# Weight sums of five groups instead of three in stage one, the first gate run's operand sums on VectorE, and another order of casts and one result copy

## The chip, the cores and the metric

The kernel runs on one core of a Trainium2 chip. The metric is the device time of one execution in microseconds. A core has five engines that run their own instruction lists in order and wait for each other by semaphores: PE (TensorE, matrix multiplication), DVE (VectorE) and POOL (GpSimd) for elementwise work, ACT (ScalarE) for functions and casts, and SP (SyncE), which here only issues DMA transfers.

## The reference, cut to what matters

```
scores = cap * tanh(q @ k^T / sqrt(64) / cap)            # 8 batches, 12 heads, 448 x 448
x  = softmax(scores) @ v   -> (8, 448, 768)
xp = x shifted by one position
k  = relu((mu_k * x + (1 - mu_k) * xp) @ w_k)            # w_k 768 x 1024
v  = (k * k) @ w_v                                       # w_v 1024 x 768
r  = sigmoid((mu_r * x + (1 - mu_r) * xp) @ w_r)         # w_r 768 x 768
out = r * v                                              # (8, 448, 768)
```

The weights come as 64-bit floats and are rounded to float32 by the kernel.

## The kernel before, in words

**Stage one** goes over 48 pairs of heads, two at a time ("units", listed in `UNIT`): scores, tanh, exp, values, the mix of positions, and between them the product with w_k (L463) whose results go through a relu (L473, tile ko) into the DRAM tensor k_d. x goes to x_d. In the same units the weights w_r and w_v are rounded, block by block: the last sum of a rounding is `weight_sum` on POOL (L548), and `weight_store` writes the block to w_d in DRAM.

**Stage two** computes the gate r and v for 14 chunks of 256 positions. Each chunk has a run "r" and a run "v". A run is a fast form of a block product with seven products instead of eight (m = 0 to 6): it needs seven sums of blocks of the operand and seven of the weights. The weights make seven groups k (0 to 2 of w_r, 3 to 6 of w_v). A group has four raw blocks of 128x384 and three more that are sums, 128x2688 in all. Where the sums are made depends on NRAW: for a group k < NRAW the four raw blocks are stored in stage one, loaded (768 KB), and summed in place by four subtractions (`group_sums`) after the load; for the others `weight_sum` writes into the tile gt, `T` makes four subtractions there on POOL in stage one, and seven blocks are stored and loaded (1344 KB). NRAW is 4 before.

After the load each group is split: `group_high` casts it to the high part on ACT (L120, 128x2688), `group_low` subtracts on DVE for the low part (L607, 128x2688). The tiles are named by letters: raw groups 0 to 6 are w2A, w2C, w2E, w2I, w2K, w2H, w2M; their high parts w2B, w2D, w2F, w2J, w2L, w2K, w2O; their low parts w2G, w2A, w2C, w2E, w2I, w2N, w2H. So the high part of group 5 (w2K) takes the place of raw group 4 and can't be written before the low part of group 4 is made from it; the low part of group 6 (w2H) takes the place of raw group 5.

**The passage between the stages** is written by hand. `LAST` lists the end of stage one and `TAIL` what is done beside the last eight blocks of the w_k product (h = 0 to 7, 18 matmuls each): `l` loads a group, `p` and `d` sum it on POOL or DVE, `c` is `group_high`, `s` is `group_low`, `@n` is the work of slot n on the first operands. A slot's work: `load_x` reads mixed positions from x_d (tile xc), `mix_r` multiplies on ACT (L662) and adds on DVE (L663) into t, `square` (L668) squares the k chunk kr, `sum1`, `sum23` and `sum4` are the four operand sums of a run, `split` casts an operand on ACT (L120, tiles ro and vo) and subtracts on DVE (L699). `chain` then goes slot by slot: `product` (L711), the slot's work, and `post`, which takes a product's result out of PSUM. The first post copies the first product (m = 4, bank ps2c) to the tile cp (L722). The third product (m = 3) adds on into the same bank, so it can't start before that copy is done. cp lies where the three ko buffers were, so the copy also waits until the last stores of ko have landed. The last ko is the relu of h = 7.

Of the kernel before, what the change touches and what calls it, by code (L numbers as in the profile page):

```python
# [57 lines left out]
LAST_R = ((-6, 4), (-3, 2), (-2, 3), (0, 0), (5, 5), (8, 1), (10, 6))  # L58
LAST_V = ((-6, 4), (-4, 2), (-3, 0), (-1, 3), (0, 5), (2, 1), (4, 6))
LAST_SPLITS = ((-8, 4), (-7, 2), (-6, 0), (-4, 3), (-3, 5), (-2, 1), (0, 6))  # L60
TAIL = ("@-12 @-11 @-10 c2 s2 p3", "@-9 @-8 c3 s3 @-7", "@-6 @-5 @-4", "open c4 s4 c5", "", "", "", "")
NRAW = 4
TAIL_TAGS = ("c0", "b0", "a0", "c1", "b1", "a1")
PAD = (24, 56)
RAW_SLOTS = "ACEIKHM"
# [22 lines left out]
k_store k_store f x_high.1 x_low.1 weight_store T T T load_vl load_v.1 x_store.0 weight_load load_qk.1 x_store.1"""  # L88
LAST = """V.0 V.1 VL next gather p0 p1 c0 recip rec_store rec_load l2 s0 c1 norm.0 norm.1 K K K relu K relu k_store
mix_old.0 mix_new.0 x_high.0 x_low.0 s1 K K mix_old.1 relu k_store K mix_new.1 x_high.1 x_low.1 relu K K relu k_store  # L90
k_store x_store.0 x_store.1 d2"""


def uncut(i):
# [3 lines left out]
def f(ap):  # L98
    return ap.bitcast(F32)


class Body:
# [441 lines left out]
    def weight_sum(self, e="p"):  # L544
        for n, a, sq in self.w_sum:
            k, q = divmod(n - NWK, 4)
            out = sq if k < NRAW else self.gt[:, q]
            {"p": self.nc.gpsimd, "v": self.nc.vector}[e].tensor_add(out, f(a), sq)  # L548
# [6 lines left out]
            else:  # L555
                if k < NRAW or q != 1:
                    self.w_done.append((k, q, out))
                if k >= NRAW:
                    self.w_block += {1: [(k, 4, 4, 1, 0)], 3: [(k, 1, 7, 3, 1), (k, 5, 5, 3, 4), (k, 6, 6, 2, 5)]}.get(q, [])
# [26 lines left out]
    def group_load(self, k):  # L586
        n = 4 if k < NRAW else 7
        self.nc.sync.dma_start(self.W[k][:, 0:n], self.w_d[k][:, 0:n])
# [86 lines left out]
        k, h = {0: (0, 0), 2: (1, 0), 3: (1, 0), 1: (0, 1), 6: (1, 1)}[m]  # L675
        return t[:, k * g:k * g + g, h * P:h * P + P]

    def sum1(self, p, c):
        if p == "r":
            self.S1[p] = self.xin.tile([P, KG[p], P], F32, name="s1")  # L680
        self.nc.gpsimd.tensor_add(self.S1[p], self.block(p, c, 1), self.block(p, c, 6))  # L681

    def sum23(self, p, c):
        a11, a21 = self.block(p, c, 0), self.block(p, c, 1)
        self.sub("p", self.S1[p], self.S1[p], a11)
        self.sub("p", a21, a11, a21)

    def sum4(self, p, c):
        a12 = self.block(p, c, 2)
        self.sub("p", a12, a12, self.S1[p])  # L690

    def split(self, p, c, m):
        a = self.block(p, c, m)
# [52 lines left out]
    def runs(self):  # L746

        runs = [(p, c) for c in range(NC) for p in "rv"]
        pe, prep = {}, {}
        for n, (p, c) in enumerate(runs):  # L750
            last = p + str(c - NC + 1)
            for rel, m in dict(r0=LAST_R, v0=LAST_V).get(last, PRODUCTS):
                pe[7 * n + rel] = (n, p, c, m)
            todo = [(-23, self.load_x, (c,)), (-12, self.mix_r, (c, 0)), (-11, self.mix_r, (c, 1)), (-10, self.mix_r, (c, 2))]
            todo = todo if p == "r" else [(-23, self.load_k, (c,)), (-12, self.square, (c, 0)), (-11, self.square, (c, 1))]
            todo += [(-9, self.sum1, (p, c)), (-7, self.sum23, (p, c)), (-5, self.sum4, (p, c))]
            todo += [(rel, self.split, (p, c, m)) for rel, m in (LAST_SPLITS if last == "v0" else SPLITS)]
            for rel, fn, a in sorted(todo, key=lambda x: x[0]):
                prep.setdefault(7 * n + rel, []).append((fn, a))
        return pe, prep  # L760
# [86 lines left out]
    def run(self):  # L847
# [8 lines left out]
        with ExitStack() as outer:  # L856
            def pool(name, bufs, stack=outer, **kw):
                return stack.enter_context(tc.tile_pool(name=name, bufs=bufs, **kw))
# [57 lines left out]
            for i in range(NSTEP):  # L916
# [22 lines left out]
                if i > NPAIR + 1:  # L939
                    for h in range(2 * (i - NPAIR - 2), 2 * (i - NPAIR - 1)):  # L940
                        n = B * NF * ND * 3 - (8 - h) * 3 * ND
                        self.kpart(n, n + 3 * ND)
                        self.relu()
                        self.k_store()
                        self.tail_work(TAIL[h])
            self.k_store()
# [9 lines left out]
            self.S1["v"] = t[:, NF * CH:NF * CH + KG["v"] * P].rearrange("p (c s) -> p c s", c=KG["v"])  # L956
            self.rsp = pool("rsp", 1, reuse_waits="tile")
            self.opp["v"] = [pool("opv0", 1, reuse_waits="tile")]
            self.tail_work("s5 c6")
            self.chain(pe, -6, -1)  # L960
            self.prep[-1].reverse()
            self.preps(-1)
            self.tail_work("s6")
# [55 lines left out]
```

## Time and profile before

| | us |
|---|---|
| median of 3 runs (lowest, highest) | 922.11 (921.96, 924.5) |
| the profiled execution | 922.12 |
| its span, first to last instruction | 919.9 |
| PE busy, of the span | 889.0 (97%) |
| DVE, ACT, POOL busy | 733.8 (80%), 619.8 (67%), 435.7 (47%) |
| PE busy in 400 to 500 | 100.00 |
| PE busy in 520 to 560 | 24.10 of 40 |
| PE busy in 700 to 800 | 99.50 |

The profiled execution took as long as the median run, and 2.2 us of it lie outside its span. PE is busy almost everywhere, except at the very start and end and in one place, between 530 and 560 us, where the kernel passes from stage one to stage two.

### The profile page before, as it was taken

The page shows a single profiled execution, that of the slowest core. Times are in us where ns is not written, and L with a number is a line of the kernel's source. Part 1 is how long each engine was busy: PE and PEld are TensorE (multiplying, and loading weights), DVE is VectorE, ACT ScalarE, POOL GpSimd, SP SyncE. Part 2 cuts the span into 40 slices and gives each one's busy share as a digit, 9 for nine tenths or more (in the row PEclk, how much of TensorE's full clock was granted, in tenths as well). Part 3 has the DMA queues.
Part 4 walks back from the last instruction along what each step waited for, and adds up shares of the span by engine and source line. Part 5 has one row for each costly group of instructions (what it writes and reads, how often), then busy time and mean ns, then how long its engine had stood idle before and what let it go on. Part 6 is the DMA issues. An engine that isn't in the chain of part 4 may idle for free.

```text
span 919.9 us, 14330 instructions
## 1 busy us (share of the span) xinstructions
PE 889.0 (97%) x5046; PEld 697.8 (76%) x5046; DVE 733.8 (80%) x1102; ACT 619.8 (67%) x957; POOL 435.7 (47%) x412
## 2 busy tenths in 40 slices
PE   7999999999999999999999948999999999999997
PEld 2335557767677776667777938999999999999997
DVE  5878987878978888897955748888888888888883
ACT  7897787788797788977973455555455555645542
POOL 2443454555555565666647614434444344334440
PEclk9999999999999999999999979999999999999999
DMA  7355565566666675666757731332333223322301
GB/s 254 115 162 179 189 193 166 190 196 186 187 217 206 191 225 179 195 206 205 211 188 235 264 116 44 115 107 83 113 107 115 79 89 115 115 88 100 107 35 47
DMA packets 96698, 140.61 MB, mean 153 GB/s; under 512 B 11496, under 2 KB 86120, under 8 KB 96232
## 3 DMA queue, kind: packets, MB, share of 16 engines
q1 hardware_dynamic: 87400, 124.91, 43.6%
q10 hardware_dynamic: 9216, 14.68, 4.2%
q8 instruction: 42, 0.69, 0.3%
q14 instruction: 40, 0.33, 0.1%
HBM read 93.00 MB, written 44.15 MB: 149 GB/s over the span
## 4 chain that ended last, share of the span: by engine, by line
PE 46%; DVE 22%; ACT 13%; issue 8%; POOL 6%; DMA 3%; SPq 1%; ACTq 0%; POOLq 0%; DVEq 0%
PE kps L463 17%; PE pv L299 10%; PE s L264 10%; DVE vo L699 3%; DVE cp L742 3%; ACT vo L120 3%; DVE ro L699 3%; DVE t L663 3%; POOL t L126 3%; PE ps2a L711 2%; ACT ro L120 2%; PE pv L308 2%; ACT t L662 2%; PE s L274 2%; PE kps L320 1%
## 5 line engine op out<-in xcount | busy, mean ns | idle before, releaser
L280 ACT ACTIVATE p<-s,scl_t 128x896 f32<-128x896 f32 x144 | 139.3, 996 | 16.3 <-PE s L264 14.4
L290 ACT ACTIVATE p<-p,cap_t 128x896 f32<-128x896 f32 x144 | 145.2, 1036 | 1.9
L463 PE MATMUL kps<-xkh,wkl 128*128 128x448 f32 x384 | 143.5, 374 | 0.8 <-ACT ko L473 0.8
L345 DVE TRANSPOSE_TENSOR_REDUCE r<-p 128x28 f32<-128x896 f32 x126 | 136.0, 1093 | 6.2 <-ACT p L290 6.0
L463 PE MATMUL kps<-xkl,wkh 128*128 128x448 f32 x384 | 140.6, 366 | 0.0
L463 PE MATMUL kps<-xkh,wkh 128*128 128x448 f32 x384 | 140.3, 365 | 0.0
L299 PE MATMUL pv<-p,rv 128*64 128x448 f32 x576 | 115.1, 544 | 0.0
L463 PEld LDWEIGHTS kps<-xkh,wkl 128*128 128x128 f32 x384 | 72.0, 188 | 26.4 <-issue 13.7
L299 PEld LDWEIGHTS pv<-p,rv 128*64 128x64 f32 x576 | 38.6, 136 | 66.4 <-issue 56.6
L548 POOL TENSOR_TENSOR wsq<-wa,wsq 128x384 f32<-128x384 f32 x32 | 34.5, 1080 | 112.7 <-DVE wsq L539 112.7
L463 PEld LDWEIGHTS kps<-xkl,wkh 128*128 128x128 f32 x384 | 72.2, 188 | 8.0 <-issue 2.8
L463 PEld LDWEIGHTS kps<-xkh,wkh 128*128 128x128 f32 x384 | 72.1, 188 | 5.8
L699 DVE TENSOR_TENSOR ro<-t,ro 128x384 fp32r<-128x384 f32 x70 | 38.7, 554 | 39.9 <-ACT ro L120 38.9
L699 DVE TENSOR_TENSOR vo<-x,vo 128x512 fp32r<-128x512 f32 x63 | 57.1, 914 | 15.9 <-ACT vo L120 15.6
L126 POOL TENSOR_TENSOR qkl<-rqk,qkh 128x832 fp32r<-128x832 f32 x34 | 67.6, 1987 | 2.8
L396 DVE TENSOR_TENSOR x<-pv,r 128x448 f32<-128x448 f32 x48 | 28.2, 620 | 42.9 <-DMA r<-rec_d 42.9
L663 DVE SCALAR_TENSOR_TENSOR t<-xc,mu_r,t 128x256 f32<-128x256 f32 (+3 forms) x120 | 57.0, 527 | 0.9
L126 POOL TENSOR_TENSOR xkl<-xk,xkh 128x448 fp32r<-128x448 f32 x48 | 55.6, 1157 | 3.9
L733 ACT ACTIVATE rs<-rs 128x384 f32<-128x384 f32 x28 | 14.7, 526 | 62.7 <-DVE rs L732 62.7
L120 ACT CAST ro<-t 128x384 fp32r<-128x384 f32 x70 | 34.4, 509 | 33.4 <-POOL t L126 33.0
L681 POOL TENSOR_TENSOR s<-t 128x384 f32<-128x384 f32 x14 | 16.9, 1205 | 75.5 <-DVE t L663 75.5
L662 ACT ACTIVATE t<-xc,om_r 128x256 f32<-128x256 f32 (+3 forms) x120 | 44.6, 435 | 3.4 <-DMA xc<-x_d 3.4
(199 smaller groups left out, 2400.8 us busy)
## 6 DMA issues: line engine op xcount, KB each, us to landing
rqk<-qk SPq DMA_DIRECT2D x47, 448.0 KB
k_d<-ko ACTq DMA_DIRECT2D x64, 224.0 KB
x_d<-x SPq DMA_DIRECT2D x48, 224.5 KB
out<-cp SPq DMA_DIRECT2D x56, 192.0 KB
rv<-v SPq DMA_DIRECT2D x48, 192.0 KB
r<-rec_d SPq DMA_DIRECT2D x36, 224.0 KB
kr<-k_d SPq DMA_DIRECT2D x7, 1024.0 KB
x<-k_d SPq DMA_DIRECT2D x7, 1024.0 KB
```

Source lines behind the costliest of these rows:

```text
L120: self.nc.scalar.copy(out, x)
L126: {"p": self.nc.gpsimd, "v": self.nc.vector}[e].tensor_sub(*a)
L264: nc.tensor.matmul(s[:, h, 0:S], qk[a][p, k], qk[b][p, 0:S], start=(n == 0), stop=(n == len(terms) - 1))
L280: self.nc.scalar.activation(p32, self.S.pop((i, g))[:, :, 0:S], AF.Tanh, scale=self.scl_t)
L290: self.nc.scalar.activation(p32, p32, AF.Exp, scale=1.0 if self.maxima else self.cap_t)
L299: nc.tensor.matmul(pv[p, 0:S], v[:, g, h, :], ph[:, h, :], start=(g == 0), stop=False)
L345: self.nc.vector.tensor_reduce(out=r1[:, :, 3 if g == "L" else g], in_=self.P32[i, g].rearrange("p h (b k) -> p (h b) k", k=32), axis=mybi ...
L463: nc.tensor.matmul(self.kps[fc][:, 0:S], w, m[:, dc, :], start=first, stop=last)
L548: {"p": self.nc.gpsimd, "v": self.nc.vector}[e].tensor_add(out, f(a), sq)
L662: nc.scalar.mul(td, self.XC[:, d, j0 + o:j1 + o], self.om["r"][:, d:d + 1])
L663: nc.vector.scalar_tensor_tensor(out=td, in0=self.XC[:, d, j0 + o + 1:j1 + o + 1], scalar=self.mu["r"][:, d:d + 1], in1=td, op0=ALU.mult, ...
L699: self.nc.vector.tensor_sub(lo, a, f(hi))
```

## The change

NRAW becomes 2, so groups 2 and 3 are summed in stage one by `T` on POOL, eight subtractions of 128x384 more there. With them go 7 blocks each instead of 4 through w_d (six stores more, 192 KB each), and their loads grow from 768 to 1344 KB. The four subtractions of group 2 on DVE (`d2`) and of group 3 on POOL (`p3`) in the passage are gone. The four operand sums of the very first run (r of chunk 0) go from POOL to DVE; all other runs keep POOL. `TAIL` is written anew: the cast of group 2 (`c2`) stands at the end of `LAST`, ahead of the mixing, `c3`, `s3`, `c4`, `c5` stand in other places, and the sums of the first run are at h = 0 to 2. The cast of group 6 (`c6`) stands behind the first product and its copy instead of ahead of them.

```
-TAIL = ("@-12 @-11 @-10 c2 s2 p3", "@-9 @-8 c3 s3 @-7", "@-6 @-5 @-4", "open c4 s4 c5", "", "", "", "")
-NRAW = 4
+TAIL = ("@-12 @-11 @-10 @-9 c3 s2 @-8", "@-7 @-6", "@-5 s3 @-4", "open c4 s4", "c5", "", "", "")
+NRAW = 2
...
-k_store x_store.0 x_store.1 d2"""
+k_store x_store.0 x_store.1 c2"""
...
-    def sum1(self, p, c):
+    def sum1(self, p, c, e):
...
-        self.nc.gpsimd.tensor_add(self.S1[p], self.block(p, c, 1), self.block(p, c, 6))
+        {"p": self.nc.gpsimd, "v": self.nc.vector}[e].tensor_add(self.S1[p], self.block(p, c, 1), self.block(p, c, 6))
...
+            e = "p" if n else "v"
+            todo += [(-9, self.sum1, (p, c, e)), (-7, self.sum23, (p, c, e)), (-5, self.sum4, (p, c, e))]
...
-            self.tail_work("s5 c6")
-            self.chain(pe, -6, -1)
+            self.tail_work("s5")
+            self.chain(pe, -6, -5)
+            self.tail_work("c6")
+            self.chain(pe, -5, -1)
```

PE's list is the same in both kernels. On ACT, at the beginning of the passage (- is before, + is the change):

```order
+L120 CAST w2F<-w2E 128x2688
 L662 ACTIVATE t<-xc,om_r 128x256 x6
-L120 CAST w2F<-w2E 128x2688
-L120 CAST ro<-s_5360 128x384
 L120 CAST w2J<-w2I 128x2688
-L473 ACTIVATE ko<-kps 128x448
-L479 DMA k_d<-ko 128x448
-L120 CAST ro<-t 128x384 x2
+L120 CAST ro<-s_5345 128x384
+L120 CAST ro<-t 128x384
+L473 ACTIVATE ko<-kps 128x448
+L479 DMA k_d<-ko 128x448
```

The cast of group 2 has moved ahead of the six multiplications of the mix, and the cast of group 3 ahead of the first operand cast; the relu of h = 2 comes after two operand casts instead of one. A little further on, the relu of h = 4 and its store move ahead of the cast of group 5 (w2K).

On ACT, at the end of the passage, where flag is the load of a register and cp the first copy out of PSUM:

```order
-L473 ACTIVATE ko<-kps 128x448
-L479 DMA k_d<-ko 128x448
-L948 TENSOR_LOAD flag
+L949 TENSOR_LOAD flag
+L722 COPY cp<-ps2c 128x384
 L120 CAST w2O<-w2M 128x2688
-L722 COPY cp<-ps2c 128x384
```

The copy now stands ahead of the cast of group 6 (w2O), and one relu fewer stands between the cast of group 5 and the copy.

On DVE, at the beginning of the passage (s and t are the operand sums and the mixed operand of the first run):

```order
 L416 SCALAR_TENSOR_TENSOR xk<-x_153,mu_k,pv 128x448
-L126 TENSOR_TENSOR w2E<-w2E 128x384 x4
 L663 SCALAR_TENSOR_TENSOR t<-xc,mu_r,t 128x256 x6
+L681 TENSOR_TENSOR s_5345<-t 128x384
 L607 TENSOR_TENSOR w2C<-w2E,w2F 128x2688
-L699 TENSOR_TENSOR ro<-s_5360,ro 128x384
+L699 TENSOR_TENSOR ro<-s_5345,ro 128x384
+L126 TENSOR_TENSOR s_5345<-s_5345,t 128x384
+L126 TENSOR_TENSOR t<-t 128x3x128
+L699 TENSOR_TENSOR ro<-t,ro 128x384
+L126 TENSOR_TENSOR t<-t,s_5345 128x3x128
+L668 TENSOR_TENSOR kr<-kr 128x1024
```

The four subtractions of group 2 are gone from DVE, and the four operand sums, which POOL did before, stand between the low part of group 2 and that of group 3. Then come the low part of group 3, the third operand, the second square and the low part of group 4, and from there DVE's list is as before: the low part of group 5, four operands, and the low part of group 6.

## Rows read from the trace of the kernel before

**Rows 1.** Windows of the passage: busy time of each engine, granted clock, DMA share, GB/s
```profile
490.00:500.00 10.00, 10.00 (x54) 7.94 (x51) 4.40 (x3) 5.21 (x3) 7.04 (x5) 1.00 0.66 180
500.00:510.00 10.00, 10.00 (x52) 9.26 (x51) 7.99 (x7) 4.17 (x10) 7.94 (x6) 1.00 1.00 363
530.00:540.00 10.00, 2.01 (x12) 1.69 (x10) 5.32 (x2) 6.06 (x5) 0.84 (x1) 0.76 0.47 160
540.00:550.00 10.00, 5.13 (x19) 5.13 (x20) 2.52 (x5) 6.44 (x11) 0.04 (x1) 0.55 0.17 66
550.00:560.00 10.00, 6.99 (x31) 6.68 (x30) 8.89 (x11) 5.26 (x13) 6.91 (x3) 0.83 0.00 1
```

**Rows 2.** Timeline of PE in the passage: start, duration, instruction [idle before, releaser]
```profile
531.67 0.34 PE L711 MATMUL ps2b<-w2F,ro 128*128 128x384 f32 x1
544.87 0.69 PE L711 MATMUL ps2c<-w2B,ro 128*128 128x384 f32 x1 [12.86 <-ACT cp L722]
...
551.02 0.34 PE L711 MATMUL ps2c<-w2N,vo 128*128 128x384 f32 x1
554.36 0.44 PE L711 MATMUL ps2c<-w2H,vo 128*128 128x384 f32 x1 [3.01 <-DVE w2H L607]
```

**Rows 3.** Timeline of ACT in the passage
```profile
505.04 2.51 ACT L662 ACTIVATE t<-xc,om_r 128x256 f32<-128x256 f32 x6 [3.38 <-DMA xc<-x_d]
...
519.08 2.44 ACT L120 CAST w2J<-w2I 128x2688 fp32r<-128x2688 f32 x1
...
529.70 2.45 ACT L120 CAST w2L<-w2K 128x2688 fp32r<-128x2688 f32 x1 [0.71 <-ACT ko L473]
535.18 2.43 ACT L120 CAST w2K<-w2H 128x2688 fp32r<-128x2688 f32 x1 [3.02 <-DVE w2I L607]
537.51 0.54 ACT L473 ACTIVATE ko<-kps 128x448 f32<-128x448 f32 x1
...
540.51 0.54 ACT L473 ACTIVATE ko<-kps 128x448 f32<-128x448 f32 x1 [0.46 <-ACT ko L473]
...
542.01 2.43 ACT L120 CAST w2O<-w2M 128x2688 fp32r<-128x2688 f32 x1 [0.95 <-ACT ko L473]
544.35 0.47 ACT L722 COPY cp<-ps2c 128x384 f32<-128x384 f32 x1
544.72 0.51 ACT L120 CAST ro<-t 128x384 fp32r<-128x384 f32 x1
...
548.53 0.62 ACT L120 CAST vo<-x 128x512 fp32r<-128x512 f32 x1
```

**Rows 4.** Chain that ended last, the step from the last ko store: start, duration
```profile
541.09 1.90 DMA k_d<-ko
```

**Rows 5.** Timeline of DVE in the passage
```profile
506.09 4.11 DVE L126 TENSOR_TENSOR w2E<-w2E 128x384 f32<-128x384 f32 x4
510.12 4.75 DVE L663 SCALAR_TENSOR_TENSOR t<-xc,mu_r,t 128x256 f32<-128x256 f32 x6
514.80 2.95 DVE L607 TENSOR_TENSOR w2C<-w2E,w2F 128x2688 fp32r<-128x2688 f32 x1
...
524.58 0.54 DVE L699 TENSOR_TENSOR ro<-t,ro 128x384 fp32r<-128x384 f32 x1
525.04 1.21 DVE L668 TENSOR_TENSOR kr<-kr 128x1024 f32<-128x1024 f32 x1
...
550.26 4.04 DVE L607 TENSOR_TENSOR w2H<-w2M,w2O 128x2688 fp32r<-128x2688 f32 x1
```

**Rows 6.** Timeline of POOL, the first operand sum
```profile
514.95 3.67 POOL L681 TENSOR_TENSOR s<-t 128x384 f32<-128x384 f32 x1 [1.55 <-DVE t L663]
```

**Rows 7.** Instructions on tile gt: nanoseconds min/median/max, first and last start
```profile
L126 POOL TENSOR_TENSOR gt<-gt x12: 997/1025/1337, 365.6 to 469.5; 128x384 f32<-128x384 f32 x12
```

**Rows 8.** Windows of two stretches of two units each in stage one, columns as in rows 1
```profile
231.30:270.71 39.41, 39.41 (x243) 27.52 (x243) 35.38 (x49) 33.06 (x40) 24.07 (x25) 1.00 0.64 199
353.24:392.65 39.41, 39.41 (x243) 27.51 (x243) 32.89 (x46) 33.52 (x41) 26.89 (x27) 1.00 0.64 200
```

More of the change, by code (lines that the diff above doesn't have):

```diff
@@ L676, in block, with sum23, sum4 @@
         return t[:, k * g:k * g + g, h * P:h * P + P]
-    def sum1(self, p, c):
+    def sum1(self, p, c, e):
         if p == "r":
             self.S1[p] = self.xin.tile([P, KG[p], P], F32, name="s1")
-        self.nc.gpsimd.tensor_add(self.S1[p], self.block(p, c, 1), self.block(p, c, 6))
-    def sum23(self, p, c):
+        {"p": self.nc.gpsimd, "v": self.nc.vector}[e].tensor_add(self.S1[p], self.block(p, c, 1), self.block(p, c, 6))
+    def sum23(self, p, c, e):
         a11, a21 = self.block(p, c, 0), self.block(p, c, 1)
-        self.sub("p", self.S1[p], self.S1[p], a11)
-        self.sub("p", a21, a11, a21)
-    def sum4(self, p, c):
+        self.sub(e, self.S1[p], self.S1[p], a11)
+        self.sub(e, a21, a11, a21)
+    def sum4(self, p, c, e):
         a12 = self.block(p, c, 2)
-        self.sub("p", a12, a12, self.S1[p])
+        self.sub(e, a12, a12, self.S1[p])
     def split(self, p, c, m):
@@ L755, in runs @@
             todo = todo if p == "r" else [(-23, self.load_k, (c,)), (-12, self.square, (c, 0)), (-11, self.square, (c, 1))]
-            todo += [(-9, self.sum1, (p, c)), (-7, self.sum23, (p, c)), (-5, self.sum4, (p, c))]
+            e = "p" if n else "v"
+            todo += [(-9, self.sum1, (p, c, e)), (-7, self.sum23, (p, c, e)), (-5, self.sum4, (p, c, e))]
             todo += [(rel, self.split, (p, c, m)) for rel, m in (LAST_SPLITS if last == "v0" else SPLITS)]
```

## The prediction

> **What bounds the kernel now.** I read the table of slices first: PE is busy in nearly every slice, with one hole. Windows of 10 us show the hole [rows 1]: PE has 2.01 us of work in 530 to 540, 5.13 in 540 to 550 and 6.99 in 550 to 560, and its clock is granted at 0.55 and 0.83 in the last two, that is, part of the time at the lower of its two levels. On both sides PE is full, so outside the hole only something that makes PE's own work longer can cost time, and inside it only what ends PE's waits can gain any.
>
> The timeline of PE says which waits these are [rows 2]. After the second product PE stops at 532.0 (531.67 + 0.34) and waits 12.86 us for the copy cp on ACT. Then it does 25 matmuls (third product, fourth product, seven of the first v product) and stops again, 3.01 us, for w2H, the low part of group 6. It goes on at 554.36, and this is the moment to follow: behind it PE hardly waits.
>
> The timeline of ACT shows why the copy is late [rows 3]. The copy itself needs a product that was ready at 532. ACT reaches it at 544.35, because the cast of group 4 (529.70), the cast of group 5 (535.18, after 3.02 us of waiting for DVE's w2I), four relus from 537.51 to 541.05 and the cast of group 6 (542.01) stand ahead of it. The chain of waits adds one more condition: the store of the last relu leaves at 541.09 and lands 1.90 us later [rows 4], and cp lies where that relu's tile was.
>
> So the hole is set by a chain of ACT and DVE that alternate over the weight groups, and it begins early: the four sums of group 2 hold DVE from 506.09 to 510.20, so the six adds of the mix end only at 514.87, although ACT had the mixed positions at 505.04 [rows 3, 5]; and the first operand sum takes POOL 3.67 us [rows 6].
>
> **The change in the passage, step by step.** All times are on the clock of the profiled execution.
>
> *Group 2 and the mix.* ACT waits 3.38 us before 505.04, so it is free from 501.66 [rows 3]; the cast of group 2 (2.44) fits in there, if its load has landed. Loads of groups 2 and 3 grow by 576 KB each. Group 2's is issued before the mixed positions xc, so xc lands later: 590 kB at 363 GB/s, the rate of 500 to 510 [rows 1], is 1.6 us, at 180 GB/s, that of 490 to 500, 3.3 us; the bounds are 0 and 3.3, since the queue was only 0.66 busy there. I take 1.6, because the next window is full: xc at 506.6. ACT's six multiplications take 2.51, to 509.2, and DVE follows one add behind: 509.7. Before it was 514.87.
>
> *Sums and low parts on DVE.* A two-input operation of 128x384 takes DVE 0.54 alone and 1.03 beside POOL (4.11/4) [rows 5]. POOL has nothing here now, so I take 0.54; the other bound adds 4 x 0.49 = 2.0 us. First sum to 510.2; low part of group 2, 2.95, to 513.2; operand 513.7 (its cast on ACT comes after the cast of group 3: 509.2 + 2.44 + 0.51 = 512.2; if group 3's load is late by the whole extra 2 x 1.6 us it may cost another 1 us); second and third sum 514.8; operand 515.4; last sum 515.9; square 1.21, 517.1; low part of group 3, 520.1; operand 520.6; square 521.8; low part of group 4, 524.8. That one ended at about 535.1 before (ACT was released at 535.18) [rows 3].
>
> *From group 5 to the copy.* The cast of group 4 on ACT follows the third operand cast (516.4) and three relus and is done by about 521, before DVE asks for it. The cast of group 5 starts when w2I is made: 524.8 to 527.2. Three relus a microsecond apart (537.51 to 540.51 is three steps) start at 527.2, 528.2 and 529.2. From the start of the last to the landing of its store it was 541.09 + 1.90 - 540.51 = 2.48 [rows 3, 4]: 531.7. The copy can start then; PE was released 0.52 after the copy's start (544.35 to 544.87): 532.2. That is 12.6 us earlier than before. If the chain were quicker by more than about 1 us, the relu of the last matmul block, which PE finishes near 528, would hold it.
>
> *From the copy to w2H.* The cast of group 6 is now behind the copy: 0.37 after it (the step 544.35 to 544.72), so at 532.1; the next operand cast comes 2.34 after that (542.01 to 544.35), at 534.4, and vo is four steps of about 0.4 later, at 536.1, since nothing in between waits for PE any more. Before, vo's cast at 548.53 was followed by w2H at 550.26, 1.73 later, and that took 4.04 [rows 3, 5]. So w2H goes from 537.8 to 541.9, and PE goes on at 541.9 instead of 554.36. The 25 matmuls in between took 6.15 us at the mixed clock (544.87 to 551.02) [rows 2]; from 532.2, with a wait for the operand of 534.4, they are over by about 540 and stay hidden. Moving the cast of group 6 back takes its 2.43 us from ahead of the copy and puts w2H 0.4 us later, no more; the cast itself stays beside PE's third product.
>
> The low part w2H took 4.04 where the same operation took 2.95 at 514.80 [rows 5]: POOL was at work beside it. The order on both engines is unchanged there, so I keep 4.04; 2.95 is the other bound (1.1 us better).
>
> **Stage one.** Eight subtractions of a median 1.025 us [rows 7] and six stores of 192 KB are added. Rows of before show the same work in later units: a stretch of two units without any work on gt, from 231.30, and one with seven operations on it, from 353.24, both take 39.41 us with 243 matmuls and a full PE, while POOL is at 24.07 and 26.89 [rows 8]. So they are hidden by PE's own work, and I cost them at nothing; the bound is 8 x 1.025 = 8.2 us, if each held PE up. A stall that is taken away from DVE in the passage reappears nowhere else before 554, for POOL's next task needs DVE's squares, which are earlier.
>
> Here a rule is weighed. POOL's first sum began at 514.95, took 3.67 and ended at 518.62, while DVE's w2C ran from 514.80 to 517.75 [rows 5, 6]: POOL did its work only after DVE let go. The Trainium skill, SBUF — State Buffer, section "SBUF: two separate sides", says that the two share a port pair as an exclusive lock: whichever starts first keeps it for its whole instruction. The trace agrees. By the rule each new subtraction in stage one may lock DVE out, 8.2 us of DVE time together; by the rows DVE has 32.89 of 39.41 us busy with seven such operations there, so PE would not feel it.
>
> **Sum.** 922.1 (the profiled execution, equal to the median) - 554.36 + 541.9 + 0 = **909.7 us**.
>
> **Rivals.**
> 1. *Operands or loads later than I think* (10 in 100). The chain from xc to w2H hands every microsecond on. The bounds of xc (3.3 - 1.6 = 1.7), of the sums (2.0) and of group 3's load (1) together give 914.4 at most; the middle is 912.5. For it: the DMA queues are full from 500 on. Against: no load but xc was waited for.
> 2. *The clock.* At 550 to 560 the granted clock of 0.83 cost 1.7 us of PE time [rows 1], after a wait of 3 us. The change still leaves a wait of some 2 to 4 us before w2H, so I assume the same loss. If PE stays at full clock: 908.0 (14 in 100); with w2H at 2.95 too: 906.9.
> 3. *Stage one stretches* (5 in 100). Each new subtraction stands in POOL's list ahead of the q and k parts of the next units, and if it is late, scores wait. At up to 8.2 us the time is 912 to 918.
> 4. *Slower than before* (3 in 100): the cast of group 2 stands at the head of ACT's list, with the mix, all casts and relus behind it. If the 1344 KB of group 2 land after 501.66, all that follows is late by as much. It turns the sign when the load is later than 12.4 + 2.8 us, after 516.9; at 20 us late the time is 930. Against it: the window from 490 on moved 1.8 MB in 10 us with a third of the queue idle.
> 5. *The gain goes elsewhere* (3 in 100): a wait behind 554 that was covered by the late w2H, such as the second chunk's loads, shows up; half of the gain gone is 916. If the copy weren't earlier at all, because the last store still sets it, the time would stay at 922 (2 in 100); but that store hangs on the relus, which move.
>
> The forecast has 63 in 100, with its own range 908.5 to 911.5. The range of 907.0 to 914.0 takes in rivals 1 and 2 and the bounds for DVE, loads and clock; about 15 in 100 lie outside, nearly all above. A difference of 0.3% (2.8 us) is about what a measurement of this kernel can tell from none; by the cases 95 in 100 are faster, 2 the same, 3 slower.
>
> **What the profile after would show.** Right: PE's wait for cp is below 2 us; the last of the six mix adds ends near 510, w2I near 525, the copy is near 532, PE's last wait for w2H ends near 542; two units in stage one still take 39.4 us. Wrong: ACT waits for w2E's load near 502; the operand sums on DVE take 1 us instead of 0.54; PE has idle time between 190 and 330; or a new wait appears on PE after 545.

## The result: 914.8 us, faster, but 5 us short of the forecast

The change takes 914.81 us (median of 4 runs, 914.48 to 915.46) against 922.52 for the kernel before on the same chip: a ratio of 0.9913, 95% interval 0.9896 to 0.9931. The direction was forecast and the size was not: the forecast was 909.7, and 914.81 lies just above its range of 907.0 to 914.0. The profiled execution took 914.52 us with a span of 912.6.

PE first. These are the windows that answer to [rows 1], of the kernel after, and under them PE's timeline, which answers to [rows 2].

```profile
530.00:540.00 10.00, 5.36 (x22) 5.03 (x21) 3.69 (x2) 5.28 (x8) 0.32 (x1) 0.75 0.52 174
540.00:550.00 10.00, 7.33 (x37) 7.01 (x37) 8.43 (x9) 5.76 (x13) 6.46 (x3) 0.91 0.00 1
550.00:560.00 10.00, 9.31 (x51) 8.40 (x50) 8.46 (x20) 6.78 (x18) 2.48 (x3) 1.00 0.26 68
```

```profile
531.70 0.34 PE L711 MATMUL ps2b<-w2F,ro 128*128 128x384 f32 x1
536.68 0.69 PE L711 MATMUL ps2c<-w2B,ro 128*128 128x384 f32 x1 [4.64 <-ACT cp L722]
...
546.29 0.44 PE L711 MATMUL ps2c<-w2H,vo 128*128 128x384 f32 x1 [2.67 <-DVE w2H L607]
...
557.96 0.44 PE L711 MATMUL ps2c<-w2B,ro 128*128 128x384 f32 x1 [0.55 <-ACT ro L120]
```

The hole is still there, smaller. The wait for cp fell from 12.86 to 4.64 us where under 2 was forecast, and PE goes on at 546.29 instead of 554.36, where 541.9 was forecast. ACT's timeline, which answers to [rows 3], shows where it went wrong; the DMA rows in it are the issues of the ko stores, with their number at the end.

```profile
502.99 2.46 ACT L120 CAST w2F<-w2E 128x2688 fp32r<-128x2688 f32 x1 [1.02 <-issue]
506.81 2.51 ACT L662 ACTIVATE t<-xc,om_r 128x256 f32<-128x256 f32 x6 [1.37 <-DMA xc<-x_d]
...
514.24 0.33 ACTq L479 DMA_DIRECT2D k_d<-ko  x1
516.74 0.51 ACT L120 CAST ro<-t 128x384 fp32r<-128x384 f32 x1 [2.53 <-DVE t L126]
517.16 0.97 ACT L473 ACTIVATE ko<-kps 128x448 f32<-128x448 f32 x2
520.45 0.55 ACT L473 ACTIVATE ko<-kps 128x448 f32<-128x448 f32 x1 [2.32 <-DMA k_d<-ko]
520.47 1.47 ACTq L479 DMA_DIRECT2D k_d<-ko  x3
521.98 2.45 ACT L120 CAST w2L<-w2K 128x2688 fp32r<-128x2688 f32 x1 [0.99 <-ACT ko L473]
526.26 0.55 ACT L473 ACTIVATE ko<-kps 128x448 f32<-128x448 f32 x1 [1.82 <-DMA k_d<-ko]
...
531.80 0.54 ACT L473 ACTIVATE ko<-kps 128x448 f32<-128x448 f32 x1 [0.46 <-ACT ko L473]
532.38 0.33 ACTq L479 DMA_DIRECT2D k_d<-ko  x1
536.15 0.48 ACT L722 COPY cp<-ps2c 128x384 f32<-128x384 f32 x1 [3.80 <-DMA k_d<-ko]
...
540.43 0.64 ACT L120 CAST vo<-x 128x512 fp32r<-128x512 f32 x1
```

Up to 516.74 the list runs about 1 us behind the forecast: the last add of the mix ended at 510.65 (forecast 509.7), the cast of group 3 waited 1.17 us for its load, and the third operand cast, forecast for about 515.9, came at 516.74. Then three waits appear that name one transfer, k_d<-ko. There are three ko tiles. At 520.45 the third relu of h = 3 stands until the store of 514.24 has landed, at 526.26 the relu of h = 4 stands on the next, and at 536.15 the copy stands on the last store. DVE hands the first of these waits on: w2I asks for the cast of group 4.

```profile
507.36 3.29 DVE L663 SCALAR_TENSOR_TENSOR t<-xc,mu_r,t 128x256 f32<-128x256 f32 x6 [0.86 <-ACT t L662]
510.69 0.56 DVE L681 TENSOR_TENSOR s<-t 128x384 f32<-128x384 f32 x1
...
521.10 1.22 DVE L668 TENSOR_TENSOR kr<-kr 128x1024 f32<-128x1024 f32 x1
524.46 2.96 DVE L607 TENSOR_TENSOR w2I<-w2K,w2L 128x2688 fp32r<-128x2688 f32 x1 [2.14 <-ACT w2L L120]
...
542.18 4.05 DVE L607 TENSOR_TENSOR w2H<-w2M,w2O 128x2688 fp32r<-128x2688 f32 x1
```

The chain that ended last gives the stores' duration (start, duration from issue to landing). It was 1.90 us in [rows 4]:

```profile
514.24 6.13 DMA k_d<-ko
532.38 3.67 DMA k_d<-ko
```

While the first of them is under way, the DMA queue is full with the loads of the groups (the last two columns of a window are the DMA share and GB/s):

```profile
514.00:516.00 2.00, 2.00 (x12) 1.85 (x11) 1.97 (x5) 0.21 (x1) 0.00 (x0) 1.00 1.08 434
518.00:520.00 2.00, 2.00 (x11) 1.86 (x10) 2.00 (x1) 0.13 (x1) 0.00 (x0) 1.00 1.12 416
```

As to the last store, SP's list has the load of k for the second chunk (1024 KB, tile x) at 528.95, and the windows around the last store have a full DMA queue.

```profile
528.95 0.38 SPq L650 DMA_DIRECT2D x<-k_d  x1
```

```profile
530.00:532.00 2.00, 2.00 (x12) 1.72 (x10) 2.00 (x1) 1.08 (x3) 0.32 (x1) 1.00 0.94 284
532.00:534.00 2.00, 0.04 (x1) 0.00 (x0) 1.13 (x1) 0.35 (x1) 0.00 (x0) 1.00 1.04 353
534.00:536.00 2.00, 0.00 (x0) 0.00 (x0) 0.00 (x0) 0.00 (x0) 0.00 (x0) 0.73 0.61 230
```

In the kernel before, the last store left at 541.09 and the windows of [rows 1] show a queue that was 0.17 busy from 540 on. The change brought the store 9 us forward, into this load.

Stage one, last, has the two stretches of [rows 8] and the rows on gt that answer to [rows 7]:

```profile
231.60:271.02 39.42, 39.42 (x243) 27.52 (x243) 34.88 (x48) 32.96 (x40) 25.33 (x26) 1.00 0.63 197
353.55:392.96 39.41, 39.41 (x243) 27.51 (x243) 34.39 (x47) 33.43 (x41) 28.44 (x28) 1.00 0.64 201
L126 POOL TENSOR_TENSOR gt<-gt x20: 995/1268/1338, 265.5 to 469.4; 128x384 f32<-128x384 f32 x20
```

There are 20 subtractions instead of 12, POOL has more to do, and two units still take 39.41 us. From 190 to 330 PE is idle for 0.34 us of 140, where it was not idle at all before.

### The profile page after: what moved, and what is told of

The parts are those of the page before. It is cut to its first block, busy times and chain, and to the rows that moved or that the text cites. A ratio compares the mean times of both kernels' runs of the same rounds, so it can differ in the third digit from the quotient of the medians.

```text
span 912.6 us, 14347 instructions
## 1 busy us (share of the span) xinstructions
PE 888.5 (97%) x5046; PEld 696.7 (76%) x5046; DVE 729.7 (80%) x1102; ACT 619.6 (68%) x957; POOL 432.8 (47%) x412
## 4 chain that ended last, share of the span: by engine, by line
PE 45%; DVE 22%; ACT 13%; issue 8%; DMA 7%; POOL 4%; SPq 1%; ACTq 0%; POOLq 0%; DVEq 0%
PE kps L463 17%; PE pv L299 10%; PE s L264 10%; DVE vo L699 3%; DVE cp L742 3%; ACT vo L120 3%; DVE ro L699 3%; POOL t L126 3%; DVE t L663 3%; ACT ro L120 2%; PE ps2a L711 2%; DMA r<-rec_d 2%; ACT t L662 2%; PE pv L308 2%; PE s L274 2%
## 5 line engine op out<-in xcount | busy, mean ns | idle before, releaser
L280 ACT ACTIVATE p<-s,scl_t 128x896 f32<-128x896 f32 x144 | 139.3, 996 | 17.5 <-PE s L264 15.4
L463 PE MATMUL kps<-xkh,wkl 128*128 128x448 f32 x384 | 143.5, 374 | 0.8 <-ACT ko L473 0.8
L463 PE MATMUL kps<-xkl,wkh 128*128 128x448 f32 x384 | 140.7, 366 | 0.0
L463 PE MATMUL kps<-xkh,wkh 128*128 128x448 f32 x384 | 140.3, 365 | 0.0
L463 PEld LDWEIGHTS kps<-xkh,wkl 128*128 128x128 f32 x384 | 72.1, 188 | 26.4 <-issue 13.0
L463 PEld LDWEIGHTS kps<-xkl,wkh 128*128 128x128 f32 x384 | 72.2, 188 | 8.0 <-issue 2.8
L463 PEld LDWEIGHTS kps<-xkh,wkh 128*128 128x128 f32 x384 | 72.1, 188 | 5.8
L699 DVE TENSOR_TENSOR vo<-x,vo 128x512 fp32r<-128x512 f32 x63 | 57.2, 915 | 13.6 <-ACT vo L120 13.3
L548 POOL TENSOR_TENSOR wsq<-wa,wsq 128x384 f32<-128x384 f32 x24 | 25.9, 1080 | 85.4 <-DVE wsq L539 85.4
L473 ACT ACTIVATE ko<-kps 128x448 f32<-128x448 f32 x64 | 32.3, 536 | 24.5 <-PE kps L463 19.2
L681 POOL TENSOR_TENSOR s<-t 128x384 f32<-128x384 f32 x13 | 13.2, 1015 | 73.9 <-DVE t L663 73.9
```

The costliest lines, as they stand in the source:

```text
L280: self.nc.scalar.activation(p32, self.S.pop((i, g))[:, :, 0:S], AF.Tanh, scale=self.scl_t)
L463: nc.tensor.matmul(self.kps[fc][:, 0:S], w, m[:, dc, :], start=first, stop=last)
L473: self.nc.scalar.activation(ko, ps[:, 0:S], AF.Relu)
L699: self.nc.vector.tensor_sub(lo, a, f(hi))
```

## The experiments

Each ratio below is to the kernel before, timed on the same chip at the same time. After itself was timed only beside its own kernel before, so where a variant is compared with after, the ratios and the profiles count for more than the medians. To compare profiles whose stage one ended at different moments, I use the **passage**: from the end of PE's last matmul of the w_k product (L463) to the start of the first matmul with w2H. It is 554.36 - 528.58 = 25.8 us in the kernel before, 546.29 - 528.88 = 17.4 after, and the forecast amounts to 541.9 - 528.58 = 13.3.

**The copy ahead of the cast of group 6, alone** (kernel before with this edit):

```
-            self.tail_work("s5 c6")
-            self.chain(pe, -6, -1)
+            self.tail_work("s5")
+            self.chain(pe, -6, -5)
+            self.tail_work("c6")
+            self.chain(pe, -5, -1)
```

> The kernel before with one part of the change: the cast of group 6 behind the first product's copy. Theory 1 (PE's last wait, for w2H, sets the end, and the copy only what comes before it): the copy can start when the last ko store has landed, at 543.0 instead of 544.35, the cast of group 6 starts at 543.4 instead of 542.0, w2H and PE's resumption come about 1.4 us later: about 923.9 us. Rival (the copy's time, PE's longest wait, is what counts): 1.3 us faster, about 921.2 us.

Measured: 922.28 us (921.19 to 923.25, 10 runs), ratio 0.999 [0.9979, 1.0]; passage 24.6. The first expectation fails, and the second holds in part: of its 1.3 us the passage shows 1.2 and the time 0.7. The copy came 2.0 us after the last store's issue instead of 544.35 - 541.09 = 3.3, and the cast behind it cost vo nothing, as I had not counted a wait: in the kernel before, the copy rs of the third product waits 2.13 us for PE, with vo behind it on ACT, and the cast now takes the place of that wait. The time moved by 0.1%, which a measurement can hardly tell from none. By itself this part of the change is worth 1 us at most.

**The weight sums in stage one, alone** (kernel before, NRAW = 2, without d2 and p3, old order of casts, operand sums on POOL):

```
-TAIL = ("@-12 @-11 @-10 c2 s2 p3", "@-9 @-8 c3 s3 @-7", ...
-NRAW = 4
+TAIL = ("@-12 @-11 @-10 c2 s2", "@-9 @-8 c3 s3 @-7", ...
+NRAW = 2
```

> The kernel before with one part of the change: the sums of groups 2 and 3 in stage one, everything else in the old order (the cast of group 2 behind the mix, operand sums on POOL). Theory 1 (the four sums on DVE from 506 to 510 and those on POOL held up a chain of casts and low parts): the mix ends 4 us earlier and the chain gets w2I by about 528.5, the copy by about 538, PE resumes at about 548: about 916 us, most of the change's gain. Rival (the larger loads take back what the sums give): 920 us or more. Stage one: two units still take 39.4 us by both.

Measured: 918.11 us (917.8 to 919.26, 5 runs), ratio 0.9945 [0.9928, 0.9962]; passage 20.6. It is over half of the whole gain. It is 2 us less than expected; what I had not counted is that the third operand cast then waits 6.06 us for POOL's last sum.

**After, with the operand sums back on POOL:**

```
-            e = "p" if n else "v"
+            e = "p"
```

> The changed kernel with the first run's operand sums back on POOL. Theory 1 (the relu of h = 3 waits until 520.45 for the landing of a ko store, and hides a later third operand): 0 to 1 us slower, about 915.2 us. Rival (the sums on DVE are what shortened the chain): 3 us slower, about 918 us.

Measured: 916.89 us (915.97 to 918.63, 4 runs), ratio 0.9931 [0.9906, 0.9955]; passage 19.6. So the move to DVE is worth about 2 us, between the two expectations; the intervals of the two ratios overlap, and the passage, 2.2 us longer than in after, says the same. POOL's timeline in this kernel shows why:

```profile
511.32 3.66 POOL L681 TENSOR_TENSOR s<-t 128x384 f32<-128x384 f32 x1 [2.35 <-DVE t L663]
516.20 1.26 POOL L126 TENSOR_TENSOR s<-s,t 128x384 f32<-128x384 f32 x1 [1.22 <-DVE ro L699]
517.43 2.00 POOL L126 TENSOR_TENSOR t<-t 128x384 f32<-128x384 f32 x1
519.39 3.73 POOL L126 TENSOR_TENSOR t<-t,s 128x384 f32<-128x384 f32 x1
```

Four sums take 10.65 us of POOL beside DVE's long subtractions, where DVE does each in 0.55.

**After, with cp away from the ko tiles** (x1, the place of the second chunk's k, lies over them instead, so that load waits for the stores and the copy does not):

```
+            t = res.tile([P, 7 * HN], F32, name="x1")
             self.CP = res.tile([P, 7, HN], F32, name="cp")
-            t = res.tile([P, 7 * HN], F32, name="x1")
...
-            self.S1["v"] = t[:, NF * CH:NF * CH + KG["v"] * P]...
+            self.S1["v"] = t[:, NF * CH + 128:NF * CH + 128 + KG["v"] * P]...
```

> The changed kernel with the places of cp and x1 exchanged, so that cp no longer lies where the ko buffers were, and the transfer of the second k chunk into x1 has to wait for the ko stores instead. Theory 1 (the copy waits 3.8 us for the landing of the last ko store, which shares the DMA queues with that transfer): the copy follows the register load at about 533.3 instead of 536.15, PE resumes at about 543.4 instead of 546.3: about 912 us. Rival (the copy is late for another reason, such as the product or the register load): no change, 914.8 us.

Measured: 911.14 us (910.76 to 912.73, 4 runs), ratio 0.9863 [0.9842, 0.9884]; passage 14.5. The copy starts 0.9 us after ACT has issued the last store, and the gain is 3.7 us. So the landing of the last store holds the copy. Whether it is slow because of the load beside it was still open, and so was the relus' wait.

**After, with the relu of h = 2 and its store ahead of the cast of group 3** (early_relu):

```
-TAIL = ("@-12 @-11 @-10 @-9 c3 s2 @-8", "@-7 @-6", "@-5 s3 @-4", "open c4 s4", "c5", "", "", "")
+TAIL = ("@-12 @-11 @-10 @-9", "", "c3 s2 @-8 @-7 @-6 @-5 s3 @-4", "open c4 s4", "c5", "", "", "")
```

> After, with the relu of h = 2 and its store ahead of the cast of group 3 instead of behind two operand casts, nothing else moved. Theory 1 (ko has three tiles and a store needs about 6 us to land while the loads of the groups fill the queues, so the third relu of h = 3 stands on the first store, and the cast of group 4 behind it): the store leaves near 511 instead of 514.2 and lands before the relu needs its tile; the cast of group 4 starts near 519.7 instead of 521.98, w2I near 522.3 instead of 524.46, the last relu near 529.7 instead of 531.80, the copy 2.1 us earlier; time 912.5 to 913. Rival (the wait is only for show, the chain is held by something else, such as the low part of group 3 or the loads): w2I still starts after 524 and the time stays at 914.5 or more. Second rival: the relus come earlier, but the landing of the last store is set by the end of the second chunk's k load, so the copy stays after 535.5 and the time is about 914.

Measured: 914.71 us (914.14 to 915.64, 4 runs), ratio 0.9908 [0.9892, 0.9925]; passage 16.9. Theory 1 fails here, for reasons that the timeline of ACT and the chain of this kernel show:

```profile
511.95 0.55 ACT L473 ACTIVATE ko<-kps 128x448 f32<-128x448 f32 x1 [2.73 <-PE kps L463]
...
512.90 2.46 ACT L120 CAST w2J<-w2I 128x2688 fp32r<-128x2688 f32 x1 [0.40 <-ACT ko L473]
```

```profile
512.53 8.34 DMA k_d<-ko
521.27 7.52 DMA k_d<-ko
534.79 2.06 DMA k_d<-ko
```

The w_k product ended 1.3 us later in this profile (530.15) than in that of after, so I count from there. The relu has to wait 2.73 us for PE, and the cast of group 3 behind it is 1.1 us later. The store leaves 3.0 us earlier, but takes 8.34 us instead of 6.13, and the third relu of h = 3 still waits. The last relu (534.22) comes 1.1 us later than in after, and the copy (536.95) all the same 0.5 us earlier, because the last store lands in 2.06 us instead of 3.67. So the last relu alone does not set the copy: how long its store takes beside the load counts as much. That points towards the second rival.

**After, with the second chunk's k load six slots later** (late_k1):

```
-            todo = ... [(-23, self.load_k, (c,)), ...
+            todo = ... [(-17 if c == 1 else -23, self.load_k, (c,)), ...
```

> After, with the load of k for the second chunk (1024 KB, it left at 528.95) six slots later in the preparation, nothing else moved. Theory 1 (the last ko store takes 3.67 us to land because it shares the queues with that load, where 1.90 was measured with empty ones): the store leaves at about 532.4 as after and lands 1.9 us later, at 534.3; the copy starts near 534.4 instead of 536.15, PE goes on near 544.5, time about 913. Rival (the landing is slow for another reason, such as the store's own place in ACT's queue): the copy stays near 536, time 914.8. Second rival (the later load is missed): PE waits for the second chunk's operand, time above 915.

Measured: 914.31 us (913.6 to 916.82, 4 runs), ratio 0.9912 [0.9892, 0.9932]. The edit does not do what its expectation assumed. Nothing stands between the two slots in SP's list, so the order of every engine is that of after, and the load left at 528.26, as PE ended the w_k product. As an experiment on the load it says nothing. As a second profile of after it says much, since here the relus happened to come earlier; these are a row of its ACT timeline and one of its chain:

```profile
536.09 0.48 ACT L722 COPY cp<-ps2c 128x384 f32<-128x384 f32 x1 [5.34 <-DMA k_d<-ko]
```

```profile
530.78 5.21 DMA k_d<-ko
```

The last store left 1.6 us earlier than in after (0.9 counted from the end of the w_k product), and the copy started at the same time (0.6 later counted from there; passage 18.0).

**Both edits together** (both_waits): 

> The edits of the two kernels above together. Theory 1 (these two landings are the whole of the miss in the chain): the last relu near 529.7, its store lands about 1.9 us later, the copy is near 532.2, within 0.5 us of the 531.7 forecast, and PE goes on near 542.4; time 910.5 to 911.5. Rival (another step of the chain takes over): copy after 534, time above 912.5.

Measured: 915.46 us (914.39 to 917.62, 4 runs), ratio 0.9924 [0.9905, 0.9943]; copy at 536.61, passage 17.1. With one edit empty and the other failed, it repeats early_relu.

**The exchange of cp and x1 with the early relu:** 

> The exchanged places of cp and x1 (the copy no longer stands on any store of ko) together with the early relu of h = 2. Theory 1: the chain before the copy is 2.1 us quicker than with the exchange alone (w2K starts near 525.3 instead of 528.4 there), so the copy stands on PE's second product near 532.1 or on the relus near 530.5, and w2H, two operand casts and the cast of group 6 behind it, comes 2 us earlier; time 909 to 909.5, against 911.1 with the exchange alone. Rival (the exchange has already taken all there is, since the copy there waited for the load of a register and not for a relu): time 910.8 to 911.3.

Measured: 911.71 us (910.98 to 913.16, 4 runs), ratio 0.9877 [0.986, 0.9894]; passage 15.8, where the exchange alone has 14.5. The early relu brings nothing here either.

**After, with the second chunk's k load issued by ACT.** This is what the six slots were meant to do:

```
-        self.nc.sync.dma_start(t, self.k_d[:, :, c * CH:(c + 1) * CH]...
+        (self.nc.scalar if c == 1 else self.nc.sync).dma_start(t, self.k_d[:, :, c * CH:(c + 1) * CH]...
```

> After, with the load of k for the second chunk issued by ACT, at its place behind the second operand cast after the copy (near 539 on after's clock), instead of by SP, which sends it as soon as PE has ended the product with w_k (528.95). Nothing else moved; ACT pays the issue, some 0.4 us ahead of vo. Theory 1 (the last ko store lands only when this load of 1024 KB, sent before it, is through the queues): the last store lands about 1.9 us after its issue, so with the relus as in after (last store 532.4) the copy starts near 534.4 instead of 536.15; PE goes on 1.3 to 1.8 us earlier, time 913 to 913.5. Rival (the landing has to do with the stores themselves, three of them a microsecond apart): the copy still comes 3.5 us or more behind the last store's issue, time 914.5 to 915.5. Second rival (the late load is missed in the second chunk): a new wait of PE behind 555, time above 915.

Measured: 912.93 us (912.3 to 914.24, 4 runs), ratio 0.9886 [0.9869, 0.9902]; passage 15.9. Theory 1 holds. In ACT's timeline and in the chain:

```profile
535.46 0.48 ACT L722 COPY cp<-ps2c 128x384 f32<-128x384 f32 x1 [2.07 <-DMA k_d<-ko]
535.58 0.38 ACTq L650 DMA_DIRECT2D x<-k_d  x1
```

```profile
533.42 1.95 DMA k_d<-ko
```

With the load out of the way the last store lands in 1.95 us, the 1.90 of [rows 4] again. The load was issued a little earlier than I expected, right behind the copy, and PE missed nothing.

**After, with the casts of groups 4 and 5 ahead of the relus that wait** (casts_first):

```
-TAIL = (..., "@-5 s3 @-4", "open c4 s4", "c5", "", "", "")
+TAIL = (..., "@-5 s3 @-4 open c4 s4", "c5", "", "", "", "")
```

> After, with the cast of group 4 (w2L) ahead of the three relus of h = 3 and that of group 5 (w2K) ahead of the relu of h = 4, so that neither cast stands behind a relu that waits for a ko tile. Theory 1 (two waits: the casts stand behind the relus, and the copy behind the queue): w2L starts near 517.2 on after's clock instead of 521.98, DVE begins w2I at 522.3 as its own work allows instead of 524.46, w2K starts near 525.3 instead of 527.46; but the copy stays between 535.5 and 536.2, since the last store lands with the end of the second chunk's k load whenever it leaves; time 914 to 915. Rival (the chain of casts alone sets the copy): it moves 1 to 2 us, time 912.5 to 913.5.

Measured: 915.21 us (914.9 to 918.58, 4 runs), ratio 0.9907 [0.9891, 0.9924]; passage 17.5, as in after. As theory 1 has it: w2I no longer waits for its cast, and all of that is lost again at the copy. The chain of this kernel (its w_k product ended at 532.60, SP sent the load at 532.68; the profiled execution was its slowest, 918.58 us):

```profile
534.27 5.59 DMA k_d<-ko
```

**These casts and the load by ACT together:** 

> The edits of the two kernels above together: casts ahead of the relus that wait, and the second chunk's k load issued late by ACT. Theory 1: the four relus follow w2K (about 527.7), a microsecond apart, the last near 530.8, its store at 531.4 lands 1.9 us later, copy near 533.4 on after's clock; 2.5 us less than after but for the issue of 0.4: time about 912.5. If the stores, sent together behind the casts, have a queue of their own making: copy after 534.5, time above 913.5.

Measured: 912.25 us (911.53 to 912.31, 4 runs), ratio 0.9874 [0.9858, 0.9891]; passage 13.8, within 0.5 of the forecast's 13.3. In its ACT timeline:

```profile
517.44 2.45 ACT L120 CAST w2L<-w2K 128x2688 fp32r<-128x2688 f32 x1
...
525.50 2.44 ACT L120 CAST w2K<-w2H 128x2688 fp32r<-128x2688 f32 x1 [4.30 <-DVE w2I L607]
...
533.46 0.48 ACT L722 COPY cp<-ps2c 128x384 f32<-128x384 f32 x1 [2.07 <-DMA k_d<-ko]
```

Taken together, the two edits undo both waits: the passage loses 3.6 us against after, 1.6 of it by the load alone. The casts gave nothing without the load and 2.0 us with it. The time shows 0.7 of these 2.0, which the timed runs hardly separate from none. Some 0.8 go with the clock at the restart: after its wait of 3.65 us for w2H, PE restarts here at the lower level (0.69 us for the first matmul, where after has 0.44), and from there to its next wait for cp (L741) it takes 565.26 - 543.57 = 21.69 us, with the load alone 566.46 - 545.58 = 20.88. The four profiles in which PE restarts at less than full clock (0.61 or 0.69 us) take 21.6 to 21.7 us for this stretch, the ten others 20.9 to 21.2. In the kernel before and in the one with the load alone the granted clock is down to 0.50 too, but only from some 2 us after the restart, and there it costs nothing; why stays open. And the w_k product ended 1.2 us later in this profile (529.76) than in that of the kernel before (528.58). With 0.5 of passage these make up the 2.5 us to the forecast's 909.7. The 1.2 may be the chip's: there the kernel before took 923.74, 1.2 more than beside the change. By ratio this kernel has 0.9874, the forecast 909.7 / 922.1 = 0.9866, inside the interval.

**The exchange of cp and x1 with these casts:** 

> The exchanged places of cp and x1 together with the casts ahead of the relus. Theory 1 (with the exchange the copy stands on ACT's own list alone, so here a quicker list counts): the last relu comes about 1 us earlier than with the exchange alone, the copy too (533.2 where it was 534.19), and w2H behind it; time about 910.2, against 911.1 with the exchange alone. Rival (ACT's list has slack there or the relus' stores wait again): 910.8 to 911.5.

Measured: 911.35 us (909.64 to 911.51, 4 runs), ratio 0.9861 [0.9845, 0.9878]; passage 12.8, the shortest of all, 1.7 less than the exchange alone. The time is that of the exchange alone. Both restart PE at the lower level; these are windows behind the resumption (the third column from the end is the granted clock) and PE's first matmul with w2H in the kernel with both edits:

```profile
544.00:546.00 2.00, 2.00 (x8) 2.00 (x7) 0.83 (x2) 1.31 (x4) 0.10 (x1) 0.50 0.00 0
546.00:548.00 2.00, 2.00 (x8) 2.00 (x8) 1.96 (x3) 1.25 (x5) 1.43 (x1) 0.50 0.02 4
```

```profile
543.02 0.69 PE L711 MATMUL ps2c<-w2H,vo 128*128 128x384 f32 x1 [3.65 <-DVE w2H L607]
```

From there to the wait for cp it is 564.69 - 543.02 = 21.67 us, and 21.68 with the exchange alone, so the clock does not explain why the shorter passage is not seen in the time. The profiled spans are 1.4 us apart (909.4 and 910.8), the timed runs don't separate the two, and why stays open.

The exchange alone and the exchange with these casts are faster than before and after: 1.4% less than before, where the change gave 0.9%.

## Why the prediction was wrong, step by step

**Group 2, the mix and the sums: right.** xc was released at 506.81 (forecast 506.6), the first sum took 0.56 (0.54), the second square ended at 521.10 + 1.22 = 522.3 (521.8); the mix, 1 us late, had caught up half of that by then. Moving the sums to DVE is worth 2 us and the group sums in stage one 4.8 (922.95 to 918.11), as measured by the two kernels that do one without the other.

**"The cast of group 4 on ACT ... is done by about 521, before DVE asks for it": wrong, 2.1 us.** It began at 521.98, since the third relu of h = 3 ahead of it waited 2.32 us for a ko tile, and DVE waited 2.14. I counted the relus by their durations and not by what they wait for. With only three tiles, a relu needs a store to have landed, and a store takes 6.13 us while the groups' loads fill the queue. In the kernel before that wait was not there: its third relu of h = 3 came 6.5 us behind the store of h = 2 (528.44 and 521.98), with the DMA share at 0.24 from 521 to 528. The kernel with casts ahead of the relus and the load late (w2I without a wait, passage 2.0 us shorter than with the load alone) shows the size. That the loads make these stores slow is read from the DMA share; no run moves them, and a fourth ko tile was not tried.

**"From the start of the last to the landing of its store it was ... 2.48": wrong, 1.8 us.** This is the term that I mis-sized. It measured 532.38 + 3.67 - 531.80 = 4.25. The 2.48 came from a store in an almost empty queue, and I moved it to a time when the next chunk's load was under way. The load by ACT shows it: 1.95 again. With the 0.5 us of smaller delays before w2I these two make up the lateness of the copy: 2.14 + 1.77 + 0.5 = 4.4, and 536.15 - 531.7 = 4.45.

The second wait hides the first. In the five profiles in which the last store leaves 1.6 to 4.6 us behind the load that SP sends and the copy waits for it (after, late_k1, early_relu, both_waits, casts_first), the copy comes 6.7 to 7.8 us behind the load: the earlier the store, the longer its landing, from 2.06 to 5.59 us. In the kernels with the sums back on POOL and with the copy moved alone, the store leaves 7.4 and 10.9 us behind the load, and lands in 1.93 and 1.90. So undoing the first wait alone brings nothing, as casts_first showed.

**From the copy to w2H: right.** 542.18 - 536.15 = 6.03 where the forecast had 537.8 - 531.7 = 6.1, and w2H took 4.05 (4.04).

**Stage one at no cost: right within what the runs show.** Units take 39.41 us as before. The end of the w_k product lay between 528.2 and 532.6 in fourteen profiles; the two of them with the stage one of before have 528.58 and 529.60, after has 528.88. A cost of up to a microsecond can't be excluded.

**The sum.** PE went on 4.39 us later than forecast. From there to the end of the span it was 366.3 us instead of 365.5, and 1.9 lay outside the span instead of 2.2: 909.7 + 4.39 + 0.8 - 0.3 = 914.6, against 914.52 of the profiled execution. The 0.8 is not settled. It is not at the wait of 0.55 for ro at 557.96, since from w2H to the wait for cp after and before take the same (20.92 and 575.25 - 554.36 = 20.89); from there to the end the profiles differ by up to 0.7 us with the same work, and before and after lie at the two ends of that.

**The rivals.** The clock of rival 2 did recover (1.00 at 550 to 560 instead of 0.83), and it gave nothing: the same 20.9 us from w2H to the wait for cp, of which PE was idle 1.04 in after and 0.36 before. So the 1.7 us that the prediction priced this clock at were not there to gain. In rival 1 the middle between 909.7 and 914.4 is 912.05, not 912.5; nothing rests on it. Rival 5 named the right place, "because the last store still sets it", and dropped it with "that store hangs on the relus, which move". The relus did move, by 9 us. The landing, whose duration I left at 1.90, moved by 6.9.

## What to carry to other kernels

The duration of a transfer belongs to the moment at which it was measured: before a small store that gates an engine is moved, look in the list of SP for what is issued around its new time, and price it by a store among such loads (6.13 us here), not by one in an empty queue (1.90). Where the tiles of a pool are few, every instruction that takes one is also a wait for an older store, and what stands behind it in its engine's list waits too. When two waits follow one another, undo both before judging either.

## What was new about the hardware

A store of 224 KB landed 1.90 to 1.95 us after its issue in an almost empty queue, in 2.06 to 5.59 us next to a load of 1024 KB, and in 6.13 to 8.37 us while loads of 1344 KB kept the DMA share at about 1.0, although ACT issued the stores and SP the loads. The Trainium skill, DMA: Bandwidth & Descriptors, section "Issuing engines are not separate DMA queues", says that transfers run on the same 16 DMA engines and interleave, whichever engine started them; the rows agree.

DVE loses by the port as POOL does. In late_k1 POOL's x sum began 10 ns ahead of DVE's low part w2N, and DVE's instruction took 4.10 us instead of 2.95; its rows:

```profile
528.33 1.29 POOL L681 TENSOR_TENSOR x<-kr 128x512 f32<-128x512 f32 x1 [20.43 <-PE kps L463]
528.34 4.10 DVE L607 TENSOR_TENSOR w2N<-w2H,w2K 128x2688 fp32r<-128x2688 f32 x1 [2.52 <-ACT w2K L120]
```

The difference is 1.15 us, about the whole of POOL's 1.29, as the exclusive lock weighed in the prediction (the Trainium skill, SBUF — State Buffer, section "SBUF: two separate sides") would have it. The 4.05 us of w2H in after look the same: POOL's sum of 541.87 began 0.31 us ahead of it and ended at 543.41. Whether a later start of that sum gives back the 1.1 us was not run.
